# Three buffers in place of two for the evacuated q and k projections (state-space convolution beside 16-head attention)

## The chip, the core and the metric

One core of one Trainium2 chip runs the kernel. The metric is the device time of one execution in microseconds, as the median of the runs shown; a profiled execution is a run of its own with its own time. PE is TensorE (matmul; PEld its weight loads), DVE VectorE, ACT ScalarE, POOL GpSimd, and SP the engine that issues the DMAs of this kernel.

## What is computed

Two independent halves, concatenated along the last axis: a long convolution with a kernel generated from a state-space model, and full softmax attention. All float32, 2048 positions, 448 channels, 16 heads of 28.

```python
# half A
dt = exp(log_dt); A = -exp(log_A_real) + 1j * A_imag          # (448, 256)
C = (C_real + 1j * C_imag) * dt[:, None]
K = 2 * einsum("dn,dnl->dl", C, exp((A * dt[:, None])[:, :, None] * pos)).real
a = irfft(rfft(u_t, 2 * L) * rfft(K, 2 * L))[:, :, :L] + u * D_skip
# half B
q, k, v = split(x @ wqkv)                                     # 16 heads, Dh = 28
p = softmax(einsum("bhqd,bhkd->bhqk", q, k) * Dh ** -0.5)
b = einsum("bhqk,bhkd->bhqd", p, v) @ wo
return concatenate([a, b], axis=-1)
```

## The kernel before

The program has two parts. The first, up to about 240 us, is the projection stage with the maxima of the first score block; its instructions are ordered by the scheduler of the framework, which takes the program's order as priority, places each instruction on its engine's queue as soon as its operands and a free buffer are there by its own reckoning, and fixes that order at compile time. Each queue (PE, DVE, ACT, POOL, SP) is then executed strictly in order on the chip: an instruction at its head that waits holds all behind it. The second part, the loop over 256 steps of attention with the convolution's work fitted in between (`for s in range(NS)`, with `ORDER` for one step), is issued in program order (`nc.kept = KEPT["a"]`).

In the projection stage two kinds of work alternate.

*Projections* (`qk_proj`, line 458; `v_proj`, line 490). The 2048 positions are cut into four chunks `c` of 512. For each chunk `transposes` turns x by PE and splits it into a high part `xh` and a rest `xl`. Then come, for each of four head groups `g` of four heads, k (`s = 1`) and q (`s = 0`), and four parts of v; in the last chunk v comes first. One projection of k or q is twelve accumulating matmuls (four pieces of the contraction, three products of high parts and rests) into one PSUM tile `pm` of 128x512. There are three such PSUM tiles in turn (`w_tile`, line 125). `evac` (line 467) empties one: ACT writes the high part into `hl[:, 0]`, DVE the difference into `hl[:, 1]`, and one DMA on SP writes both to `k_d` or `q_d` in HBM. For k of the first two chunks it also makes the difference of the two halves (`kb`, `dhl`: ACT, DVE, ACT, POOL) and writes it to `kd_d`. In the traces these are the instructions `hl<-pm` on ACT and DVE and the DMAs `k<-hl`, `q<-hl` and `kd<-dhl`. The program emits the evacuation of one projection behind the matmuls of the next (`project`, line 532).

*Seeds* (`seeds(o)`, line 315, eight blocks `o`). They prepare the powers from which the convolution's kernel is generated. One block loads four parameter pieces (`nat`), scales and transposes them (`pn`), makes exponentials and sines on ACT (`tri`, with changes of the activation table), products on POOL and DVE (`qhat`, `sg`, `px`, `gz`, `x_e`), and writes its result to HBM by two DMAs, `sd<-sg` and `sd<-qhat`. The blocks use the three `qhat` buffers in turn, so POOL's clearing of such a buffer for block o + 3 (`MEMSET qhat`) waits for the write of block o.

At the end of the stage k of group 0 is read back as `khat` into the space of the weights (`load_k`, line 145), the k differences as `kdif`, and q as `qhat` (`load_q`, line 165). These loads stand on SP's queue among the last evacuations' writes. Sixteen blocks of `max_mm` (line 173) then find the first maxima, with one matmul on `kdif` and three on `khat` each; the first of them is the matmul `pt<-kdif,qhat`.

The names of the tile pools matter for one thing: `x_p.tile(..., name="hl", bufs=2)` gives tiles of this name two places in SBUF in turn, so the third tile waits until the first has been read by its DMA.

Of the kernel before, what the change touches and what calls it, by code (L numbers as in the profile page):

```python
# [9 lines left out]
F32R = mybir.dt.float32r  # L10
# [14 lines left out]
CQ = 512  # L25
# [65 lines left out]
def body(ctx, tc, a, out):  # L91
# [5 lines left out]
    def pool(stack, name, bufs=1, space=None, side=None):  # L97
        kw = {} if space is None else {"space": space}
        if side:
            kw["side"] = side  # L100
        return stack.enter_context(tc.tile_pool(name=name, bufs=bufs, reuse_waits="tile", **kw))
# [23 lines left out]
    def w_tile():  # L125

        n_ring[0] += 1
        return ps_w[0].tile([128, CQ], F32, name=f"pm{n_ring[0] % ps_w[1]}")
# [83 lines left out]
    with ExitStack() as st:  # L212
# [3 lines left out]
        x_p = pool(xst, "x_p")  # L216
# [241 lines left out]
        def qk_proj(c, s, g):  # L458
            pp = w_tile()
            n = 0  # L460
            for k in range(NCK):
                for i, x_ in ((0, xh), (1, xh), (0, xl)):
                    nc.tensor.matmul(pp, w_g[:, i, s, k, g].rearrange("p h e -> p (h e)"), x_[k],
                                     start=n == 0, stop=n == 3 * NCK - 1)
                    n += 1

            def evac():
                hl = x_p.tile([128, 2, CQ], F32R, name="hl", bufs=2)
                th, tl = hl[:, 0], hl[:, 1]
                if s == 1:  # L470
                    nc.scalar.activation(th, pp, AF.Identity, bias=kones)
                    nc.vector.scalar_tensor_tensor(tl, pp, kones, th.bitcast(F32), op0=ALU.add, op1=ALU.subtract)
                else:
                    nc.scalar.activation(th, pp, AF.Copy)
                    nc.vector.tensor_tensor(tl, pp, th.bitcast(F32), ALU.subtract)
                if s == 1 and c < 2:
                    HC = CQ // 2
                    kb = y_p.tile([128, HC], F32, name="kb")
                    dhl = y_p.tile([128, 2, HC], F32R, name="dhl")
                    dh, dl = dhl[:, 0], dhl[:, 1]  # L480
                    nc.scalar.activation(kb, pp[:, HC:], AF.Copy)
                    nc.vector.tensor_tensor(kb, pp[:, :HC], kb, ALU.subtract)
                    nc.scalar.activation(dh, kb, AF.Copy)
                    nc.gpsimd.tensor_tensor(dl, kb, dh.bitcast(F32), ALU.subtract)
                    nc.sync.dma_start(kd_d[g][:, :, c * HC:(c + 1) * HC].rearrange("i p l -> p i l"), dhl.bitcast(F32))
                nc.sync.dma_start((k_d[g][:, :, c * CQ:(c + 1) * CQ] if s == 1 else q_d[g][c]).rearrange("i p l -> p i l"),
                                  hl.bitcast(F32))
            return evac
# [651 lines left out]
```

## Time and profile before

| what | value |
|---|---|
| median of 3 runs | 1292.87 us (1292.81 to 1293.53) |
| the profiled execution's own time | 1296.34 us |
| its span, first to last instruction | 1294.3 us, 33256 instructions |
| PE busy | 1228.1 us (95%) |
| ACT busy | 956.6 us (74%) |
| DVE busy | 933.2 us (72%) |
| POOL busy | 847.0 us (65%) |
| granted PE clock, mean | 0.976 |
| DMA moved | 205.36 MB, mean 159 GB/s |

The page divides the span into 40 slices; PE is at 90% or more from the ninth to the last but one, and the first eight slices, where it falls to 50 to 90% in most, are where the projections, the seeds and the first maxima lie. All instructions carry the line of one helper, so groups are told apart by the tiles' names. Of a timeline row the first number is the start, the second the duration or, for merged rows, the stretch; a bracket tells for how long the engine was idle before it and what ended that.

### The profile page before, as it was taken

The page shows a single profiled execution, that of the slowest core. Times are in us where ns is not written, and L with a number is a line of the kernel's source. Part 1 is how long each engine was busy: PE and PEld are TensorE (multiplying, and loading weights), DVE is VectorE, ACT ScalarE, POOL GpSimd, SP SyncE. Part 2 cuts the span into 40 slices and gives each one's busy share as a digit, 9 for nine tenths or more (in the row PEclk, how much of TensorE's full clock was granted, in tenths as well). Part 3 has the DMA queues.
Part 4 walks back from the last instruction along what each step waited for, and adds up shares of the span by engine and source line. Part 5 has one row for each costly group of instructions (what it writes and reads, how often), then busy time and mean ns, then how long its engine had stood idle before and what let it go on. Part 6 is the DMA issues. An engine that isn't in the chain of part 4 may idle for free.

```text
span 1294.3 us, 33256 instructions
## 1 busy us (share of the span) xinstructions
PE 1228.1 (95%) x12625; PEld 703.1 (54%) x12625; DVE 933.2 (72%) x2106; ACT 956.6 (74%) x2142; POOL 847.0 (65%) x728
## 2 busy tenths in 40 slices
PE   7979885899999999999999999999999999999997
PEld 5767762455555555555555555555555555554433
DVE  5778876878777787787788888888888655645111
ACT  4878762488888888888888888888887766656552
POOL 2466571398888788888769999998996222424321
PEclk9889887899999999999999999999999999999999
DMA  6677779736765546468634132742425443647655
GB/s 193 229 261 253 245 235 289 210 73 145 181 147 137 125 139 166 131 164 237 177 95 111 48 87 52 164 108 68 103 51 155 154 152 133 202 151 243 201 163 169
DMA packets 200088, 205.36 MB, mean 159 GB/s; under 512 B 95992, under 2 KB 158520, under 8 KB 197880
## 3 DMA queue, kind: packets, MB, share of 16 engines
q1 hardware_dynamic: 199928, 203.23, 55.7%
q8 instruction: 100, 1.64, 0.5%
q14 instruction: 60, 0.49, 0.1%
HBM read 120.73 MB, written 82.18 MB: 157 GB/s over the span
## 4 chain that ended last, share of the span: by engine, by line
PE 76%; DVE 9%; POOL 5%; ACT 4%; issue 3%; DMA 3%; SPq 0%; ACTq 0%; POOLq 0%; DVEq 0%
PE pm L75 43%; PE pss L75 16%; PE po L75 16%; DVE mx L75 2%; ACT tri L75 1%; POOL e L75 1%; DVE rl L75 1%; DMA khat<-k 1%; POOL qhat L75 1%; DVE tri L75 1%; DVE px L75 1%; DVE sg L75 1%; DVE qhat L75 1%; POOL p L75 1%; PE pt L75 1%
## 5 line engine op out<-in xcount | busy, mean ns | idle before, releaser
L75 ACT ACTIVATE p<-pss 128x512 f32<-128x512 f32 x1024 | 561.2, 611 | 112.1 <-PE pss L75 107.6
L75 PE MATMUL pss<-qhat,khat 128*128 128x512 f32 x1024 | 403.1, 400 | 1.5 <-ACT p L75 1.4
L75 DVE TENSOR_REDUCE mx<-pm 128x1 f32<-128x512 f32 x500 | 321.7, 684 | 109.2 <-PE pm L75 107.0
L75 PE MATMUL pm<-khat,qhat 128*128 128x512 f32 x749 | 327.1, 440 | 3.3 <-DVE mx L75 2.1
L75 POOL TENSOR_TENSOR e<-e,sdb 128x256 f32<-128x256 f32 x168 | 201.9, 1202 | 118.6 <-ACT e L75 109.3
L75 PE MATMUL po<-p,v 128*32 128x512 f32 x2048 | 269.4, 594 | 0.0
L75 POOL TENSOR_TENSOR e<-e,eu 128x256 f32<-128x256 f32 x168 | 248.1, 1477 | 13.2
L75 PEld LDWEIGHTS pm<-khat,qhat 128*128 128x128 f32 x749 | 141.9, 190 | 199.1 <-ACT p L75 48.6
L75 DVE CUSTOM_DVE_ANT_0 rl<-pm,rl 128x512 f32<-128x512 f32 x249 | 171.5, 689 | 65.6 <-ACT rl L75 62.0
L75 PEld LDWEIGHTS pss<-qhat,khat 128*128 128x128 f32 x1024 | 190.7, 189 | 45.7 <-issue 10.8
L75 POOL TENSOR_TENSOR eu<-e,sdb 128x256 f32<-128x256 f32 x168 | 201.9, 1202 | 0.0
L75 POOL TENSOR_TENSOR p<-pr,pr 64x448 f32<-64x448 f32 x64 | 73.1, 1143 | 159.5 <-PE pm L75 134.0
L75 ACT ACTIVATE rl<-pm 128x512 f32<-128x512 f32 x249 | 151.2, 607 | 20.9 <-PE pm L75 20.9
L75 DVE TENSOR_TENSOR g<-g,zg 128x128 f32<-128x128 f32 x392 | 162.2, 414 | 3.4
L75 PE MATMUL pm<-xh,khat 112*128 112x512 f32 x256 | 90.3, 434 | 14.1 <-DVE hl L75 7.1
L75 PE MATMUL pm<-kdif,qhat 128*128 128x512 f32 x249 | 101.3, 407 | 2.4 <-DVE mx L75 1.3
L75 DVE TENSOR_TENSOR zg<-g,zg 128x128 f32<-128x128 f32 x224 | 87.9, 393 | 5.1
L75 PEld LDWEIGHTS pm<-e,g 128*32 128x32 f32 x3584 | 57.2, 109 | 43.8 <-issue 16.4
L75 DVE TENSOR_TENSOR pr<-pm,ub 128x448 f32<-128x448 f32 x64 | 37.0, 620 | 56.4 <-PE pm L75 42.0
L75 PE MATMUL pm<-e,g 128*32 128x64 f32 x3584 | 73.0, 222 | 1.9 <-POOL e L75 1.9
L75 ACT ACTIVATE y<-pm 128x448 f32<-128x448 f32 x48 | 26.5, 553 | 58.1 <-PE pm L75 34.0
L75 PEld LDWEIGHTS pm<-xh,khat 112*128 112x128 f32 x256 | 52.5, 209 | 29.0 <-DVE hl L75 8.6
(134 smaller groups left out, 1446.0 us busy)
## 6 DMA issues: line engine op xcount, KB each, us to landing
sdb<-sd SPq DMA_DIRECT2D x56, 336.0 KB
khat<-k SPq DMA_DIRECT2D x64, 256.0 KB
qhat<-q SPq DMA_DIRECT2D x64, 256.0 KB
sd<-sg SPq DMA_DIRECT2D x8, 1456.0 KB
k<-hl SPq DMA_DIRECT2D x16, 512.0 KB
q<-hl SPq DMA_DIRECT2D x16, 512.0 KB
mw<-in_mw SPq DMA_DIRECT2D x16, 512.0 KB
sd<-qhat SPq DMA_DIRECT2D x8, 896.0 KB
```

The source lines that it names most:

```text
L75: i = f(*args, **kw)
```

## The change

The tile that takes the evacuation of a k or q projection gets three places in SBUF in place of two. Nothing else in the text of the kernel changes.

```diff
             def evac():
-                hl = x_p.tile([128, 2, CQ], F32R, name="hl", bufs=2)
+                hl = x_p.tile([128, 2, CQ], F32R, name="hl", bufs=3)
                 th, tl = hl[:, 0], hl[:, 1]
                 if s == 1:
                     nc.scalar.activation(th, pp, AF.Identity, bias=kones)
```

The same instructions are issued, with one more 4 KB tile per partition. The scheduler takes the third buffer into account, so the fixed order of the queues differs as well, on all five engines, but only in the projection stage; the order of the loop is the same.

## Prediction

> **What bounds the kernel now.** I read the page first, then the windows in time order, then the waits and the timelines around the tile that the edit touches. Times are microseconds from the span's start. The windows list, for each stretch, its length, then the busy time of PE, PEld, DVE, ACT and POOL with counts, the granted clock, the DMA engines' busy share and GB/s.
>
> ```profile
> span 1294.3 us, 33256 instructions
> ```
>
> ```profile
> 80.00:100.00 20.00, 14.29 (x59) 12.08 (x60) 12.76 (x26) 14.30 (x34) 10.60 (x17) 0.74 0.88 303
> 100.00:120.00 20.00, 17.39 (x79) 13.89 (x78) 16.72 (x33) 16.07 (x43) 11.52 (x15) 0.91 0.81 277
> 120.00:140.00 20.00, 17.85 (x80) 14.26 (x79) 18.07 (x35) 14.42 (x33) 16.96 (x21) 0.91 0.72 259
> 140.00:160.00 20.00, 18.11 (x84) 16.20 (x83) 15.64 (x29) 17.93 (x51) 7.25 (x10) 0.83 0.56 185
> 160.00:180.00 20.00, 19.03 (x89) 15.18 (x88) 18.39 (x33) 17.60 (x43) 16.00 (x18) 1.00 0.83 275
> ...
> 200.00:220.00 20.00, 11.86 (x30) 6.55 (x30) 13.50 (x30) 5.28 (x11) 0.00 (x0) 0.71 1.05 297
> ...
> 400.00:1294.00 894.00, 878.69 (x10109) 471.95 (x10109) 627.28 (x1452) 674.04 (x1489) 605.15 (x475) 1.00 0.50 139
> ```
>
> From 400 on PE is busy 878.69 of 894: the attention loop is bound by PE, is issued in a written order, and does not contain the edited tile. The edit can only move the moment at which that loop begins; what the stage before it gains or loses reaches the end whole. In the projection stage PE has holes (14.29 of 20 at 80 to 100), but DVE and ACT are 78 to 92% and 72 to 90% busy between 100 and 180, so no single engine bounds it; it is a race of dependent chains.
>
> What the edited tile costs there, from the view of the instructions that write or read it:
>
> ```profile
> its engine sat idle before it (us, times) until:
> ...
>   DMA k<-hl: 7.9, 2
>   DMA q<-hl: 7.7, 4
> ```
>
> These 15.6 us are ACT waiting, before it writes the high part, for the write-out of the evacuation two earlier, which still holds the buffer. With three buffers the write-out waited for is one evacuation older. In the trace every one of the six waits is for the nearer one.
>
> **First place: the wait near 80.** Timeline rows (start, duration, engine; in brackets the idle time before and its releaser), from the answers for ACT, SP, POOL and PE:
>
> ```profile
> 78.61 0.81 ACT L75 ACTIVATE hl<-pm,kones 128x512 fp32r<-128x512 f32 x1
> 84.33 0.60 ACT L75 ACTIVATE hl<-pm 128x512 fp32r<-128x512 f32 x1 [4.92 <-DMA q<-hl]
> 78.58 1.96 POOL L75 TENSOR_TENSOR dhl<-kb,dhl 128x256 fp32r<-128x256 f32 x1
> 80.57 0.36 SPq L75 DMA_DIRECT2D kd<-dhl  x1
> 81.03 0.41 SPq L75 DMA_DIRECT2D q<-hl  x1
> 85.70 0.74 PE L75 MATMUL pm<-vh,xh 112*128 112x448 f32 x1 [5.94 <-DVE hl L75]
> ```
>
> The write of q stands on SP behind the write of the k differences, which waits for POOL until 80.54; so q's write starts at 81.03, lands just before 84.33, and ACT stands 4.92 us in front of the next evacuation. Everything queued behind it on ACT (the table load and sines of the seeds) waits too, and PE, with three PSUM tiles, stops for 5.94. In the new order of SP this write stands ahead of that kd write, and the evacuation of group 2's q waits instead for group 1's k, long out. So 4.92 us of the hole go; about 1.0 of PE's 5.94 stays. This is the gross value, A = 4.9.
>
> How much of A lives on to the end of the stage? PE idles 20 - 17.39, 20 - 17.85, 20 - 18.11 and 20 - 19.03 = 7.6 us in the four windows from 100 to 180, and DVE is busy 68.8 of those 80. To keep 4.9, DVE would have to do its 68.8 in 75.1 (92%, its level at 160 to 180). Bounds: 0 (the later chains eat it) and 4.9. Nearest row: DVE at 120 to 140 does 18.07 of 20, 90%, which would fit 68.8 into 76, saving 4; but POOL and ACT chains interleave with it, so I take half, A = 2.5.
>
> **Second place: the end of the stage.** The compiled order of the two programs differs on all engines within this stage and not in the loop. The part that matters: before, group 1's last q evacuation stood on DVE behind the last seeds block's sine product; now it stands in front of three products (two of which used to precede it), and on ACT in front of the last sine.
>
> ```profile
> 178.56 1.20 DVE L75 TENSOR_TENSOR sg<-tri 128x336 f32<-128x336 f32 x1
> ...
> 180.56 0.49 DVE L75 TENSOR_TENSOR sg<-tri 128x336 f32<-128x336 f32 x1
> ...
> 181.27 1.03 DVE L75 TENSOR_TENSOR sg<-tri 128x336 f32<-128x336 f32 x1
> 182.22 0.55 DVE L75 TENSOR_TENSOR sg<-sg,px 128x224 f32<-128x224 f32 x1
> 184.49 0.51 DVE L75 TENSOR_TENSOR sg<-tri 128x336 f32<-128x336 f32 x1 [1.72 <-ACT tri L75]
> 185.54 0.57 DVE L75 TENSOR_TENSOR sg<-pn,tri 128x224 f32<-128x224 f32 x1 [0.55 <-POOL tri L75]
> 185.95 0.68 DVE L75 TENSOR_TENSOR hl<-pm,hl 128x512 fp32r<-128x512 f32 x1
> ```
>
> ```profile
> 179.28 1.25 ACT L75 ACTIVATE tri<-tri 128x1232 f32<-128x1232 f32 x1
> ...
> 183.15 1.30 ACT L75 ACTIVATE tri<-tri,half_pi 128x1232 f32<-128x1232 f32 x1
> ```
>
> ```profile
> 186.66 0.38 SPq L75 DMA_DIRECT2D q<-hl  x1
> ...
> 188.50 1.98 SPq L75 DMA_DIRECT2D khat<-k  x4
> 190.59 0.39 SPq L75 DMA_DIRECT2D k<-hl  x1
> ...
> 192.75 0.64 SPq L75 DMA_DIRECT2D q<-hl  x1
> ```
>
> ```profile
> 180.00:184.00 4.00, 1.47 (x7) 0.85 (x5) 2.77 (x6) 1.67 (x3) 2.74 (x3) 1.00 0.72 247
> 184.00:188.00 4.00, 1.31 (x3) 1.12 (x4) 2.01 (x4) 3.97 (x13) 3.47 (x8) 0.51 0.11 42
> ```
>
> ```profile
> 186.69 1.22 PE L75 MATMUL pm<-xh,khat 112*128 112x512 f32 x2 [5.22 <-DVE hl L75]
> ...
> 191.50 0.63 PE L75 MATMUL pm<-xh,khat 112*128 112x512 f32 x2
> ...
> 206.94 0.76 PE L75 MATMUL pt<-kdif,qhat 128*128 128x512 f32 x1 [12.47 <-DMA khat<-k]
> ```
>
> DVE works without a hole up to 182.77 and then waits for the sine and for POOL. In the new order the evacuation starts when that run ends less two of the three products: 182.77 minus 1.52 to 2.23, so 180.5 to 181.3 in place of 185.95. ACT can supply its high part in time, since it now follows the sine that ended before 179.28. The write of q then issues near 181.9, 4.7 us sooner, and with it the loads behind it in SP's queue: khat and qhat, for which PE waits until 206.94. From 200 on the DMA share is 1.05: these transfers run back to back, so an earlier start helps only by DMA time now idle before 188, that is 4 x 0.28 + 4 x 0.89 = 4.7 us, the same figure. What is late next: group 2's k still waits on DVE behind the sine product, so its write moves only from 190.59 to about 187.4 (DVE's 185.54 + 0.57, one product of 0.5, the evacuation's 0.7), 3.2 us, and q's behind it likewise. Bounds of B: 0 and 4.7; I take 4.0, between these two delays.
>
> PE's 5.22 us hole goes with it, but PE is not what ends the stage there. The clock was 0.51 at 184 to 188 and two matmuls took 1.22 us against 0.63 at 191.50; cold time lies ahead of the loads that decide, so I count it at 0. [...]
>
> **The other waits.** Of the 15.6, 10.7 remain.
>
> ```profile
> 196.84 0.69 ACT L75 ACTIVATE hl<-pm,kones 128x512 fp32r<-128x512 f32 x1 [6.50 <-DMA k<-hl]
> ```
>
> The longest, 6.50, ends at 196.84, where transfers already in SP's queue and not ACT decide the time: 0. The other four, 4.2 together, are short beside the holes that other waits leave on ACT; bounds 0 and 4.2, I count 0. Against this stands the new order itself: the first seeds block's sines come two evacuations later; on SP the loads of the seeds' parameters move behind evacuation writes in five of seven blocks, and writes of finished seeds too (rival 2). They are issued up to five writes later, under 1 us of issue each by the 0.36 to 0.64 of such writes above; I charge 0.5, bounds 0 and 5 (rival 2's price). SBUF grows by one 4 KB tile per partition and no loop instruction is reordered: 0.
>
> **Sum.** 2.5 + 4.0 - 0.5 = 6.0 us less. The profiled execution took 1296.34 us (span 1294.3 and 2.0 around it); its sum is 1290.3. The runs shown have a median of 1292.87, 3.5 lower, so the forecast is 1287 for them.
>
> **Rivals.** (1) *Nothing arrives*, 1293. DMA at 1.05 from 200 on, with the same bytes, speaks for it: if the transfers of the sixth seeds block are still in flight at 181, khat gains nothing, and A is eaten. Against it: the share of 0.11 at 184 to 188.
>
> (2) *Slower*, 1298: the seeds' chain becomes late. In the new order the write of the third seeds block stands on SP behind a k write:
>
> ```profile
> 104.56 0.36 SPq L75 DMA_DIRECT2D sd<-qhat  x1
> ...
> 123.62 0.36 SPq L75 DMA_DIRECT2D k<-hl  x1
> ```
>
> ```profile
> 108.77 0.52 POOL L75 MEMSET qhat<- 128x112 f32 x2 [0.85 <-DMA sd<-qhat]
> ...
> 129.59 0.99 POOL L75 TENSOR_TENSOR tri<-tri 128x224 f32<-128x224 f32 x1 [1.60 <-ACT tri L75]
> ```
>
> POOL clears a seeds tile only when that write has landed (4.2 us after issue here) and now does so directly ahead of the product of 129.59. Issued at 124.0 it lands at 128.2, cleared by 128.7: just in time. It decides as soon as the k write is issued over 0.9 us later than now relative to the seeds; at 6 us later POOL, and DVE and ACT behind it, lose 5.1, the tail gains nothing, and the time is 1298.
>
> (3) *All of it*: A 4.9, PE's remaining 1.0, B 4.7 and 1.4, a third of the small waits, 12 us, 1281. For it: idle time on every engine at 80 to 100; against it: DVE's 92%.
>
> That the change frees nothing isn't a rival of weight: the waits name this tile.
>
> **How the numbers follow.** Forecast (3 to 9 us gained) 0.44; all of it 0.13; nothing, within 0.2% (2.6 us, about what a measurement can tell from no change), 0.17; slower 0.26, since a reordered stage of so many chains can lose as easily as it gains. Faster 0.57, same 0.17, slower 0.26. The likeliest case alone spans 1284 to 1290. The range leaves out most of the all-of-it case's far end and the upper part of the slower one: 1280 to 1298.
>
> **What would show it.** In the new profile: the waits of ACT for k and q writes before 189 gone; PE's hole near 80 under 2 us; group 1's q evacuation on DVE about 5 us before the last sine product; the first matmul on kdif at 199 to 203; the loop after 400 unchanged in length. It is wrong if POOL's wait for the seeds' writes grows from its present level, if the first matmul on kdif is not before 206, or if the loop itself changes.

## The result, and the profile after

| | median | ratio to before, 95% interval |
|---|---|---|
| before | 1293.13 us (1292.81 to 1293.53, 4 runs) | |
| after | 1284.6 us (1284.39 to 1285.01, 4 runs) | 0.9935, 0.9923 to 0.9947 |

The third buffer saves 8.5 us; the forecast was 1287 us, about 6 saved. The profiled execution after took 1284.77 us. The line of its page with the span, and one line of its windows (columns as in the prediction's):

```profile
span 1283.0 us, 33256 instructions
```

```profile
400.00:1283.00 883.00, 867.00 (x9965) 465.61 (x9965) 618.39 (x1432) 664.42 (x1466) 593.72 (x466) 1.00 0.51 139
```

PE is still busy 98% of the time from 400 on. The first matmul of the attention loop, `pss<-qhat,khat`, starts at 246.80 before and at 234.70 after; from there to the end of the span it is 1047.5 and 1048.3 us. So the whole gain lies ahead of the loop, as the prediction said. (The two starts lie 12.1 us apart and the medians 8.5, because the profiled execution of before was a slow one, with 1296.34 us; in a second profile of before, further down, the loop starts at 242.10 and takes 1047.2.)

The windows of the projection stage after:

```profile
20.00:40.00 20.00, 19.14 (x86) 14.50 (x86) 15.10 (x43) 12.88 (x34) 2.63 (x4) 1.00 0.67 240
...
80.00:100.00 20.00, 16.88 (x83) 14.12 (x81) 17.97 (x35) 17.70 (x44) 13.69 (x16) 0.92 0.82 276
100.00:120.00 20.00, 19.64 (x89) 15.18 (x88) 17.20 (x32) 18.39 (x44) 13.74 (x18) 1.00 0.86 302
120.00:140.00 20.00, 15.86 (x86) 13.80 (x86) 18.01 (x35) 17.14 (x43) 14.81 (x21) 0.95 0.75 251
140.00:160.00 20.00, 19.16 (x87) 15.95 (x87) 17.43 (x30) 17.47 (x48) 13.39 (x19) 0.88 0.69 216
160.00:180.00 20.00, 15.71 (x65) 12.05 (x65) 16.59 (x32) 15.64 (x37) 12.35 (x17) 0.97 0.90 297
```

From 80 to 120 DVE and ACT are fuller than before (17.97 and 17.70 against 12.76 and 14.30 in the window from 80), and the chunks that follow are done earlier: the first k evacuation of the fourth is at 157.89 in place of 168.04.

The view of the instructions that write or read the edited tile, after:

```profile
its engine sat idle before it (us, times) until:
  DMA k<-hl: 6.9, 2
  ACT hl L75: 6.0, 4
  PE pm L75: 3.1, 5
```

Six waits for writes of k and q (15.6 us) have become two (6.9). The larger of the two, 5.47, stands near the end of the stage where the last one stood before (6.50).

At the end of the stage, timeline rows of after (DVE, then SP's queue, then PE):

```profile
171.81 0.68 DVE L75 TENSOR_TENSOR hl<-pm,hl 128x512 fp32r<-128x512 f32 x1
...
176.15 0.56 DVE L75 TENSOR_TENSOR sg<-pn,tri 128x224 f32<-128x224 f32 x1 [0.57 <-POOL tri L75]
```

```profile
173.27 0.52 SPq L75 DMA_DIRECT2D q<-hl  x1
...
176.14 1.98 SPq L75 DMA_DIRECT2D khat<-k  x4
```

```profile
194.86 0.76 PE L75 MATMUL pt<-kdif,qhat 128*128 128x512 f32 x1 [11.25 <-DMA khat<-k]
```

Group 1's q evacuation now runs 4.3 us ahead of the last sine product (`sg<-pn,tri`, the one released by POOL), where it ran 0.4 behind. The loads of khat start 0.01 us ahead of that product, where they started 188.50 - 185.54 = 3.0 behind it.

And the place near 80, after (ACT, POOL, PE):

```profile
77.27 0.38 ACT L75 ACTIVATE kb<-pm 128x256 f32<-128x256 f32 x1 [4.70 <-POOL dhl L75]
77.55 0.59 ACT L75 ACTIVATE hl<-pm 128x512 fp32r<-128x512 f32 x1
```

```profile
75.53 1.02 POOL L75 TENSOR_TENSOR x_e<-qhat 128x336 f32<-128x336 f32 x1
76.51 0.72 POOL L75 TENSOR_TENSOR dhl<-kb,dhl 128x256 fp32r<-128x256 f32 x1
```

```profile
78.17 1.22 PE L75 MATMUL pm<-xh,khat 112*128 112x512 f32 x2 [4.35 <-DVE kb L75]
```

The wait for q's write (4.92) is gone, but ACT now stands 4.70 us in front of `kb`, the helper of the k difference. It has a single buffer; its last reader is POOL's `dhl<-kb,dhl` at 76.51, which stands on POOL behind the seeds' products. PE's hole has shrunk only from 5.94 to 4.35. POOL's waits for the writes of finished seeds blocks shrink as well: three before (4.23, 7.17 and 0.85 us, ending at 60.30, 87.71 and 108.77), one after (5.07, ending at 60.43). The 7.17 belongs to the same place: that seeds write stands on SP at 81.50, right behind that write of q.

### The profile page after: what moved, and what is told of

It reads as the page before. It is cut to its first block, busy times and chain, and to the rows that moved or that the text cites. A ratio compares the mean times of both kernels' runs of the same rounds, so it can differ in the third digit from the quotient of the medians.

```text
span 1283.0 us, 33256 instructions
## 1 busy us (share of the span) xinstructions
PE 1221.8 (95%) x12625; PEld 696.6 (54%) x12625; DVE 931.8 (73%) x2106; ACT 957.1 (75%) x2142; POOL 844.4 (66%) x728
## 4 chain that ended last, share of the span: by engine, by line
PE 75%; DVE 11%; ACT 4%; POOL 4%; issue 3%; DMA 2%; SPq 0%; POOLq 0%; ACTq 0%; DVEq 0%
PE pm L75 42%; PE pss L75 16%; PE po L75 16%; DVE mx L75 2%; POOL e L75 1%; ACT tri L75 1%; DVE sg L75 1%; DVE tri L75 1%; DVE rl L75 1%; DVE px L75 1%; DVE hl L75 1%; DMA khat<-k 1%; DVE qhat L75 1%; POOL p L75 1%; DMA tri<-in_B_wqkv 1%
## 5 line engine op out<-in xcount | busy, mean ns | idle before, releaser
L75 DVE TENSOR_TENSOR g<-g,zg 128x128 f32<-128x128 f32 x392 | 162.2, 414 | 3.4
L75 PE MATMUL pm<-xh,khat 112*128 112x512 f32 x256 | 86.9, 421 | 13.7 <-DVE hl L75 5.2
L75 ACT ACTIVATE ub<-pm 128x224 f32<-128x224 f32 (+1 forms) x96 | 38.8, 449 | 39.7 <-PE pm L75 37.4
```

The source lines that it names most:

```text
L75: i = f(*args, **kw)
```

## The experiments

To compare profiles, I measure five points of each from the start of its own first `hl<-pm,kones` on ACT (between 19.5 and 21.3 us into the span, which varies from run to run): the first k evacuation of the second, third and fourth chunk, the sine product of the last seeds block (its first `sg<-pn,tri`, the one that POOL releases; a second one follows later), and the first matmul on kdif. The last column but one is the time from sine product to that matmul.

| kernel | 2nd | 3rd | 4th | sine | kdif | sine to kdif | median us |
|---|---|---|---|---|---|---|---|
| before, first profile | 40.49 | 91.23 | 147.15 | 164.65 | 186.05 | 21.40 | 1293.13 |
| before, second profile | 39.57 | 87.33 | 142.32 | 159.80 | 181.25 | 21.45 | |
| after | 35.65 | 84.78 | 137.64 | 155.90 | 174.61 | 18.71 | 1284.6 |
| only chunk 0 | 35.65 | 87.04 | 138.74 | 156.02 | 179.30 | 23.28 | 1288.97 |
| only chunk 1 | 40.60 | 87.12 | 140.68 | 158.15 | 181.38 | 23.23 | 1289.81 |
| only chunk 2 | 39.57 | 88.80 | 143.31 | 159.81 | 181.72 | 21.91 | 1291.29 |
| only chunk 3 | 39.58 | 90.43 | 145.22 | 161.54 | 179.23 | 17.69 | 1288.45 |
| chunks 0 to 2 | 35.68 | 84.86 | 137.74 | 155.34 | 178.25 | 22.91 | 1288.5 |
| two buffers, late write | 39.57 | 90.09 | 145.26 | 162.76 | 180.23 | 17.47 | 1289.12 |
| one evacuation | 37.55 | 87.97 | 143.68 | 159.84 | 181.91 | 22.07 | 1291.49 |
| that one and chunk 3 | 37.56 | 88.52 | 143.45 | 160.34 | 178.09 | 17.75 | 1287.67 |

Up to the fourth chunk, four of these programs have the order of before on PE, ACT, DVE and POOL (both profiles of before, "only chunk 3", "late write"); their means are 39.8, 89.8, 145.0, and 162.2 at the sine product. Against these after is ahead by 4.2, 5.0, 7.3 and 6.3 (against the fastest of them by 3.9, 2.6, 4.7 and 3.9), and the distance from sine to kdif adds 2.7 (21.4 to 18.71).

**The kernel before, a second time.** No edit.

> The kernel of before, unchanged, profiled a second time. If the first profile's 3.5 us over the median lay in the projection stage, as the profile of the kernel with the third buffer in the last chunk alone suggests (its third chunk starts at 109.97 under the same order, 112.12 in the first profile), the first matmul on kdif comes near 203.5 in place of 206.94, and the loop keeps its length. If the excess lies in the loop, it comes at 206.9 again.

One run took 1291.32 us, with a span of 1289.3. The order being the same, the 3.9 us between the two profiles at the third chunk (91.23 and 87.33) is what this stage varies by itself. So single profiles cannot settle a term of 3 us; medians and the distances within one profile (21.40 and 21.45 from sine to kdif) can.

**The third buffer in one chunk at a time.** The tile's name is chosen from a ring of three in chunk c = 0 (or 1, 2, 3), of two elsewhere (`n_hl = [-1]` is set ahead of `qk_proj`):

```diff
-                hl = x_p.tile([128, 2, CQ], F32R, name="hl", bufs=2)
+                n_hl[0] = (n_hl[0] + 1) % (3 if c == 0 else 2)
+                hl = x_p.tile([128, 2, CQ], F32R, name=f"hl{n_hl[0]}")
```

> Third buffer in the first chunk alone, two in the others. Theory A (gains made early in the stage add up to the end): the first chunk's last q evacuation came 4.6 us earlier in the changed kernel's profile than in the first profile of before (46.12 to 41.55), of which up to 3.5 may be that profile's own slowness; so 1 to 4 us faster than before, the middle 2.5. Rival (the seeds' chains eat every early gain, and only the last chunk counts): 0, within 1 us.

> Third buffer in the second chunk alone. The prediction's term A put 2.5 us (at most 4.9) here, at the wait near 80. The changed kernel's profile shows ACT standing 4.70 us at the same place for POOL's low part of the k differences instead; if that wait takes the other one's place whole, this gives 0 to 1 us. The rival, the prediction's own step: 2.5 us faster or more.

> Third buffer in the third chunk alone. Between the third chunk's first evacuation and the last chunk's first one the changed kernel gained 3.1 us in the profiles (112.12 to 105.03, then 168.04 to 157.89). Theory A: 2 to 3 us faster from this chunk by itself. Rival: the gain there is a consequence of the earlier start of the seeds, and this chunk alone gives under 1 us.

> Third buffer in the last chunk alone; only the orders of DVE and ACT differ from before. The prediction's term B: 4.0 us faster (bounds 0 and 4.7). In the changed kernel's profile the first matmul on kdif came 12.07 us earlier and the last seeds block's sine product only 9.39, so this chunk would give 2.7. Rival (the transfers run back to back and the earlier start is worth nothing): 0.

Measured beside before at 1292.99 (1291.01 to 1297.02, 19 runs): chunk 0 0.9966 (0.9954 to 0.9978), chunk 1 0.9968 (0.9955 to 0.9981), chunk 2 0.9984 (0.9973 to 0.9996), chunk 3 0.9964 (0.995 to 0.9978). By the medians that is 4.0, 3.2, 1.7 and 4.5 us, 13.4 in all, where all four together give 8.5. The intervals reach some 1.5 to 1.8 us to either side of each, so the order of the four among themselves is not settled, but the sum's excess is clear of them.

Chunk 3 is the prediction's term B. The distance shows it: from the sine product to the first matmul on kdif it takes 17.69 us instead of 21.4, and the sine product itself comes no earlier than with two buffers (161.54, against 159.80 and 164.65). Rows of "only chunk 3" (DVE, PE):

```profile
174.13 0.67 DVE L75 TENSOR_TENSOR hl<-pm,hl 128x512 fp32r<-128x512 f32 x1
...
181.08 0.57 DVE L75 TENSOR_TENSOR sg<-pn,tri 128x224 f32<-128x224 f32 x1 [0.55 <-POOL tri L75]
```

```profile
198.77 0.77 PE L75 MATMUL pt<-kdif,qhat 128*128 128x512 f32 x1 [11.02 <-DMA khat<-k]
```

Chunk 1 holds the prediction's term A, and alone it behaves as foreseen. Rows of "only chunk 1" (ACT, PE):

```profile
77.33 0.51 ACT L75 ACTIVATE kb<-pm 128x256 f32<-128x256 f32 x1
77.59 0.74 ACT L75 ACTIVATE hl<-pm 128x512 fp32r<-128x512 f32 x1
```

```profile
79.92 0.73 PE L75 MATMUL pm<-xh,khat 112*128 112x512 f32 x2 [1.05 <-DVE kb L75]
```

No wait on ACT at this place, and 1.05 of the hole left on PE, which is the 1.0 that the prediction kept; 3.2 us arrive from the chunk as a whole. The wait for `kb` that stands there in the changed kernel does not arise.

Chunk 0 entered the sum only through the charge of 0.5 for the new order, and is worth 4.0. What happens there, before (second profile) on ACT:

```profile
28.70 1.71 ACT L75 ACTIVATE nat<-nat,dt_all 56x256 f32<-56x256 f32 x4 [3.32 <-DVE dt_all L75]
30.32 0.67 ACT L75 ACTIVATE hl<-pm,kones 128x512 fp32r<-128x512 f32 x1
```

and after:

```profile
23.14 0.69 ACT L75 ACTIVATE hl<-pm,kones 128x512 fp32r<-128x512 f32 x1
...
28.39 1.71 ACT L75 ACTIVATE nat<-nat,dt_all 56x256 f32<-56x256 f32 x4 [0.51 <-DVE dt_all L75]
```

With two buffers the scheduler places the evacuation of group 1's k behind the scaling of the seeds' parameters, and that scaling stands 3.32 us waiting for a chain of small DVE operations (most of them 0.17 to 0.20 us each, up to `dt_all`). No wait names `hl` there: the buffer was reckoned with when the order was made, and in the trace only its consequence is seen. The window of the same stretch in the second profile of before, against 19.14 and a clock of 1.00 above:

```profile
20.00:40.00 20.00, 16.48 (x70) 11.83 (x69) 15.02 (x41) 12.23 (x32) 3.54 (x3) 0.91 0.59 202
```

PE does 16.48 of 20 there in place of 19.14, and the second chunk begins 3.9 us later.

Chunk 0 also settles what happens near 80. Rows of "only chunk 0", which has two buffers there, on ACT:

```profile
78.71 0.38 ACT L75 ACTIVATE kb<-pm 128x256 f32<-128x256 f32 x1 [3.28 <-POOL dhl L75]
78.99 0.59 ACT L75 ACTIVATE hl<-pm 128x512 fp32r<-128x512 f32 x1
```

The 4.92 us wait is gone without a third buffer in chunk 1, and the wait for `kb` (3.28) stands in its place, as in the changed kernel (4.70). With the third buffer everywhere the write of q stands on SP at 67.69, ahead of the write of the k differences at 77.26; before, it stood behind it (81.03 and 80.57). SP's queue of "only chunk 0" is not shown.

**Chunks 0 to 2 together, and the transfers of the end in the kernel before.** The first has `3 if c != 3 else 2` in the ring. The second keeps two buffers and moves the 1456 KB write of the seventh seeds block (`sd<-sg`), whose data are read back only later, behind the loads of khat, qhat and v on SP (called the late write here):

```diff
-                slots[max(SP * o + (i or -2), 0)] += st_
+                slots[37 if (o, i) == (6, 11) else max(SP * o + (i or -2), 0)] += st_
```

> Three buffers in chunks 0 to 2, two in the last chunk; the order up to the last chunk is that of the changed kernel, the order of the last chunk that of the kernel before. Theory that the gain has two parts, one that arises before the last chunk (sine product of the last seeds block 4.9 us earlier) and one that arises in it (3.7 us): the sine product near 176.2 as in the changed kernel, the first matmul on kdif 21.4 us later as before, 197.6, and a median near 1288.2, 4.9 below the kernel before. Rival, the transfers of the tail set the end whatever the last chunk does: the first matmul on kdif near 195 and a median near 1285, as in the changed kernel. Rival, the gains of the chunks add up: 4.2 + 3.3 + 1.8 = 9.3 us, a median near 1284.

> The kernel before (two buffers) with only the 1456 KB write of the seventh seeds block moved behind the loads of khat and qhat on SP. Theory, in the kernel before the last chunk is set by the late q write and not by the transfers up to about 184, and by the transfers only from about 190 on, ahead of which this write still stands at 188.96: most of its 4 to 4.8 us come back, first matmul on kdif near 198.5, median near 1289. Rival, the chain through the sines and the last k write (195.8) sets the end by itself and the transfers have slack: under 1 us, 1292.5. In the changed kernel the same move gave 4.0 us.

Beside before at 1292.98 (1289.6 to 1296.27, 20 runs): chunks 0 to 2 at 1288.5, 0.9966 (0.9955 to 0.9978); two buffers with the late write 1289.12, 0.997 (0.996 to 0.9981). So the gain has two parts that add up: 4.5 us from the first three chunks and 4.5 from the last, 9.0 against 8.5 together. The sum agrees within the intervals. Within the first part hardly anything adds up: by the medians chunk 0 alone gives 4.0 us and all three 4.5, and at the sine product chunk 0 alone stands at 156.02, all three at 155.34, after at 155.90. What chunk 1 or 2 can win alone is largely won by chunk 0 already; for the wait near 80 the rows above show it, for chunk 2 it was not traced. By these profiles the lost 4.4 us (4.0 + 3.2 + 1.7 - 4.5) are lost ahead of the sine product and not in the transfers of the end.

Those transfers bound the end nevertheless, in both kernels: the late write saves 3.9 us here and 4.0 in the changed kernel, below. The windows of after show them back to back:

```profile
172.00:176.00 4.00, 4.00 (x18) 3.00 (x16) 1.83 (x4) 4.00 (x11) 1.00 (x2) 1.00 1.05 372
176.00:180.00 4.00, 1.04 (x3) 0.83 (x3) 2.79 (x5) 3.25 (x6) 3.00 (x9) 0.86 1.01 275
180.00:184.00 4.00, 3.61 (x11) 2.45 (x10) 2.51 (x8) 0.00 (x0) 2.49 (x3) 0.71 0.97 274
184.00:188.00 4.00, 0.00 (x0) 0.00 (x0) 2.58 (x6) 1.17 (x3) 3.64 (x4) 0.72 1.06 310
188.00:192.00 4.00, 0.00 (x0) 0.00 (x0) 1.29 (x3) 0.56 (x2) 0.00 (x0) 0.50 1.08 373
```

The DMA share is 0.97 to 1.08 in each; the hole of 0.72 and 0.11 that the prediction meant to fill is full. A quicker start of the last chunk is partly given back, probably for that reason: with two buffers in it, the distance from sine to kdif grows from 21.4 to 22.9 and 23.3 when the sine is 6 to 7 us earlier.

**The new wait, and the late write, in the changed kernel.** First, `kb` and `dhl` of the changed kernel are put into tiles that are free at that time (`kb` gets two buffers, `dhl` one for each group):

```diff
-                    kb = y_p.tile([128, HC], F32, name="kb")
-                    dhl = y_p.tile([128, 2, HC], F32R, name="dhl")
+                    kb = kd_p.tile([128, CQ], F32, name="rl", bufs=2)[:, :HC]
+                    dhl = kd_p.tile([128, CQ], F32R, name=f"kdif{g}").rearrange("p (i l) -> p i l", i=2)
```

Second, the late write as above, with three buffers. Third, both.

> Three buffers for the evacuations, and besides the k differences' two small tiles get more places (two and four, in space that later tiles use), so that ACT near 72 to 77 need not wait for POOL. Theory: the 4.70 us wait that took the place of the old one goes, the second chunk ends about 3 us earlier, and 1 to 3 us of it reach the end: 1282 to 1284. Rival: the end of the stage is bound by the transfers, which run back to back from 164 on in the changed kernel: within 1 us of the changed kernel, 1284 to 1285.5.

> Three buffers, and the 1456 KB write of the seventh seeds block moved on SP behind the loads of khat, of the second qhat and of v; no other queue changes. Theory (the end of the stage is bound by transfers, whose engines are full from 164 to 226): the first matmul on kdif comes earlier by that write's time, 1456 KB at some 300 GB/s, 4.8 us, and the kernel is 3 to 5 us faster than the changed one, 1280 to 1281.5. Rival (ACT, DVE or POOL decide there): no change, 1284 to 1285.5.

> Both of these at once. If the two causes are independent and the transfers hide the second chunk's gain in the first place, this is faster than the sum of the two alone: 1277 to 1280. If the seeds' chains decide after all, it is no faster than the better of the two.

Beside before at 1293.14 (1291.23 to 1294.04, 7 runs): free helper tiles 1282.12 us, 0.9917 (0.9902 to 0.9932); late write 1280.59, 0.9906 (0.9891 to 0.9921); both 1278.94, 0.9901 (0.9884 to 0.9918), the fastest version here. The first, at the place near 80 (ACT, where `rl` now stands for `kb`, and PE):

```profile
74.75 0.38 ACT L75 ACTIVATE rl<-pm 128x256 f32<-128x256 f32 x1 [1.47 <-DVE hl L75]
```

```profile
75.72 0.73 PE L75 MATMUL pm<-xh,khat 112*128 112x512 f32 x2 [1.16 <-DVE rl L75]
```

The 4.70 us wait and all but 1.16 of PE's hole are gone, and the third chunk starts 2.5 us earlier than after (82.28 against 84.78 from the first evacuation). The median is 2.5 lower, though the two intervals overlap, and 2.5 us at the third chunk is less than what that point varies by from profile to profile (3.9). So the wait is gone, and what it had cost is 2.5 us at best estimate, not clear of noise; beside the late write the same tiles give 1.7 (1280.59 to 1278.94, intervals overlapping again). Both together are about the sum of the two alone (1284.6 - 2.5 - 4.0 = 1278.1), not faster than it, so the transfers had not hidden a gain of the second chunk. The late write makes the first matmul on kdif wait for another transfer and brings it 3.5 us forward:

```profile
191.33 0.76 PE L75 MATMUL pt<-kdif,qhat 128*128 128x512 f32 x1 [6.23 <-DMA qhat<-q]
```

**One evacuation alone.** Does the whole lead of chunk 0 come from the evacuation that is moved from 30.3 to 23.1? It alone gets a buffer of its own, and the second kernel adds a ring of three in chunk 3:

```diff
-                hl = x_p.tile([128, 2, CQ], F32R, name="hl", bufs=2)
+                if (c, s, g) == (0, 1, 1):
+                    hl = x_p.tile([128, 2, CQ], F32R, name="hl2")
+                else:
+                    n_hl[0] = (n_hl[0] + 1) % 2
+                    hl = x_p.tile([128, 2, CQ], F32R, name=f"hl{n_hl[0]}")
```

> One single evacuation, k of group 1 in the first chunk, gets a buffer of its own; the 31 others share two. ACT then has this evacuation in front of the scalings of the seeds' parameters, which wait for dt_all, in place of behind them (29.79 to 30.32 in the kernel before, 23.1 in the changed one). Theory, the lead of chunk 0 comes from this one place: first k evacuation of the second chunk near 56 (60.8 before), the last sine product near 176 to 178, a median near 1289, as with three buffers in the whole of chunk 0 (1288.97). Rival, the lead needs the third buffer at the later evacuations of chunk 0 too: first k evacuation of the second chunk near 60, a median of 1292 to 1293.

> The third buffer for that one evacuation and for the eight of the last chunk, two buffers elsewhere. Theory, these two places carry the whole gain and the third buffer in the second and third chunk adds nothing: 4.0 + 4.5 = 8.5 us, first matmul on kdif near 195, a median near 1284.6, as the changed kernel. Rival, the wait near 80 (ACT in front of a q evacuation for the write of an earlier q) is worth its 2.5 us beside them, since it is there again with two buffers in the second chunk: a median near 1287.

Beside before at 1292.95 (1290.99 to 1296.69, 15 runs): 1291.49, 0.9984 (0.9974 to 0.9993), and 1287.67, 0.995 (0.9936 to 0.9963). My theory fell here: by the medians the one evacuation brings 1.5 us of the 4.0 of chunk 0 (the two intervals overlap only at 0.9974 to 0.9978), and the second kernel stays 3.1 us above the 1284.6 that the theory gave. Rows of the first kernel on ACT:

```profile
23.67 0.69 ACT L75 ACTIVATE hl<-pm,kones 128x512 fp32r<-128x512 f32 x1
...
41.73 0.67 ACT L75 ACTIVATE hl<-pm,kones 128x512 fp32r<-128x512 f32 x1
...
91.53 0.69 ACT L75 ACTIVATE hl<-pm,kones 128x512 fp32r<-128x512 f32 x1 [3.36 <-DMA k<-hl]
```

The evacuation is at its early place, but that of group 3's k comes 20.95 us after the first one, against 37.73 - 20.25 = 17.48 after: with two buffers it stands behind a table load and the first long `tri<-tri` of the seeds. So half of the lead (1.9 of 3.9 at the second chunk) is gone before chunk 1, and waits for writes come again there (3.36 in the last row). With chunk 3 added the sum holds: 1.5 + 4.5 = 6.0 expected from the parts, 5.3 measured. This is the rival's 1287, but not for its reason: the 4.92 us wait near 80 is not there in that kernel's trace; ACT waits 3.08 and 3.40 us for writes of k instead. Which later evacuations of chunk 0 bring the rest was not tested.

## Why the prediction was right, step by step

- *The bound, and that only the time ahead of the loop can move.* Right: 1047.5 and 1048.3 us from the loop's first matmul on.
- *B = 4.0, the last chunk.* Right in mechanism and size: 4.5 us alone (0.9964, 0.995 to 0.9978), and 3.7 to 4.2 in the distance from sine to kdif (21.4 to 17.69; 22.91 to 18.71). The DMA engines are full after (a share of 0.97 to 1.08 from 172 to 192), as the argument on their idle time ahead of 188 had it. PE's hole of 5.22 us there did not go, though the prediction said it would; it shrank to 2.96 (at 179.08 after) and does not end the stage.
- *A = 2.5, the wait near 80.* The wait went as said, but the step "about 1.0 of PE's 5.94 stays" failed in the changed kernel: 4.35 stays, since ACT stands there for the single buffer of `kb`. In chunk 1 alone the step is right (1.05 left, 3.2 us gained). But the third buffer in chunk 0 removes the 4.92 us wait by itself and brings the one for `kb` (3.28 in "only chunk 0"), so beside chunk 0 the third buffer in chunks 1 and 2 adds only 0.5 us (1288.97 to 1288.5). The prediction asked what is late next for B and not for A. Its row was also one of the longer ones: in the second profile of before the same wait is 3.44.
- *Other waits 0, new order a charge of 0.5.* This is the mis-sized term. The new order of the first chunk is a gain of 4.0 us alone, and with A's place it makes the 4.5 of the first three chunks, for which the sum had 2.5 - 0.5 = 2.0. The 2.5 us difference is what the forecast missed. That the total still came near is partly luck: the 2.0 was expected from the place near 80, and nearly all of the 4.5 comes with chunk 0, which the sum had as a loss. For B it is not luck. The prediction looked for the tile's cost in the waits that name it; in chunk 0 the missing buffer had cost time through an order fixed at compile time.
- *The clock counted at 0.* In the windows from 20 to 40 it is 0.91 before (second profile) and 1.00 after, and 0.50 again at 188 to 192 after, where PE is idle (0.00 of 4). The mean of the eight windows of 20 us from 20 to 180 is 0.96 in the second profile of before and 0.95 after (0.90 in the first profile), and from 180 to 200 it is 0.67 and 0.60 (0.77). So against the second profile the clock explains hardly any of the gain, and counting it at 0 holds. Neither of the two holes of PE that the prediction names was removed, 4.35 and 2.96 us of them are left, so what such a hole costs by the clock was not shown.
- *What would show it.* Held: group 1's q evacuation 4.3 us ahead of the sine product (about 5 said), the loop unchanged, and POOL's waits for seeds' writes, whose growth would have spoken against it, down in sum from 12.25 us to 5.07 (the first alone is longer, 5.07 against 4.23). Not held: two waits for k's writes remain before 189 (1.48 and 5.47), and PE's hole near 80 is 4.35. The first matmul on kdif came at 194.86, ahead of the 199 to 203 named, because of chunk 0 and because the profile from which the figure was counted spent some 4 us more in this stage than the second one did (202.50 there against 206.94).
- *The rivals.* (1) Nothing arrives: no, but the end is bound by transfers as it said, which the late write's 3.9 and 4.0 us show. (2) POOL late on the third seeds block's write: no; the clearing of that buffer (121.60, and the next one at 141.20) waits for nothing after:

```profile
121.60 0.55 POOL L75 MEMSET qhat<- 128x112 f32 x2
141.20 0.51 POOL L75 MEMSET qhat<- 128x112 f32 x2
```

(3) All of it, 12 us: not by this edit; with the `kb` wait removed and the write moved as well it is 14.2 us.

## What to carry to other kernels

Where a scheduler fixes the order at compile time, a buffer that is missing costs in two ways: in waits that name it (4.92 us near 80), and in an order made around it, whose waits name something else (3.32 us for `dt_all`); compare the orders from the first difference on, not only at the named waits. Before a removed wait is booked as gained, look for the next single-buffered tile in the same chain (here `kb`). Here the gains of one chain overlapped (8.9 us one at a time, 4.5 together), while the gains on both sides of a common point added up (4.5 and 4.5 to 8.5).

## What was not expected of the hardware

The projection stage varies by itself: with the same order of PE, ACT, DVE and POOL the third chunk starts 87.33, 90.09, 90.43 and 91.23 us after the first evacuation, while the second chunk is reached within 39.57 to 40.49 in all four. Part of it shows near 80: POOL's last two operations ahead of the write of the k differences (`qhat<-qhat,x_e` and `dhl<-kb,dhl`) take 1.02 and 1.31 us in the fastest of the four and between 1.50 and 1.68, and 1.95 and 1.96, in the others, and ACT's wait for q's write is 3.44 us there against 4.92 in each of the others. Why POOL is slower there, and where the rest arises, was not traced. And one write of 1456 KB placed behind the loads that are waited for was worth 3.9 and 4.0 us, about half as much as the change itself, though PE's long wait there (11.25 after, 12.47 before) names only the load of khat.
